# Attention with two expert layers on one core: the second layer's output product in a seven-product block form, made inside the next tile's steps, with part of the weights read from DRAM for every tile

## The chip, the core and the metric

The kernel runs on one core of a Trainium2 chip. The core has TensorE (PE in the tables, with its weight loads as PEld), VectorE (DVE), ScalarE (ACT), GpSimd (POOL), and SyncE (SP), which here only issues transfers. The metric is device microseconds of one execution.

## The reference

```python
# attention: 4 batches, 8 heads, 768 positions, head size 64 (local window plus a few global keys)
x = attention(q, k, v)                               # 3072 tokens x 512
h = maximum(maximum(x @ w1, x @ w2), x @ w3)         # 512 -> 768
x2 = h @ w_out                                       # 768 -> 512
gate = 1 / (1 + exp(-(x2 @ w_gate)))                 # 512 -> 1536
val = x2 @ w_val                                     # 512 -> 1536
out = (gate * val) @ w2_out                          # 1536 -> 512
```

Inputs and output are wide floats. The kernel computes each product with both operands split into two 16-bit parts (high and low), so that one product is three matmuls: high x high, low x high, high x low.

## The kernel before

The first phase does the attention, the first layer, and the conversion of all weights; the result x2 goes to DRAM. The second phase (`phase2`) does the second layer in 6 tiles of 512 tokens, and each tile in 6 steps f, each of which makes 256 of the 1536 middle columns.

A step makes gate and value in the seven-product form of a 2 x 2 block product (Strassen's, in Winograd's arrangement; the table `WINO` names which of seven weight blocks meets which of seven input blocks). The function `prod(n)` in `phase2` makes one of the seven: 12 matmuls of 256 columns into one PSUM bank (2 sides, 2 halves of the contraction, 3 split terms), 84 a step. The products 6, 5, 7, 2, 3, 4 take turns in three banks with the tag `mm`; product 1 has one bank `pv`. VectorE adds each bank into buffers in SBUF (`add`, line 763; seven such additions a step), and a bank is free for the third next product when its addition is done. Then ScalarE makes the sigmoid (790, 794), VectorE multiplies by the value (791, 795), and `split` (line 229) makes the two 16-bit parts: ScalarE casts to the high part (234), VectorE subtracts it to get the low one (243).

The output product is plain: `out_step` adds one step's share into four banks (`tr`, `sc`), with 2 x 4 x 3 = 24 matmuls of 512 columns, and it is placed in the step after. After a tile's sixth step ScalarE scales the four banks (736) and SyncE stores them.

`load_x2` (line 688) makes the seven input blocks of a tile from x2: seven splits and four subtractions (698) of 512 elements on VectorE, seven casts on ScalarE. There are two such buffers, so tile t+2 can be split only when the last matmul of tile t is done. The weights of the second layer are converted in the first phase (`w2_steps`), written to DRAM, and read back once; all 6 steps' weights stay in SBUF for the whole second phase.

The order of the instructions on each engine is made by the framework: it lists them by its own model of their times and emits each when its inputs are ready in that model. On the chip every engine runs its list strictly in that order.

Of the kernel before, what the change touches and what calls it, by code (L numbers as in the profile page):

```python
# [8 lines left out]
F32 = mybir.dt.float32  # L9
# [34 lines left out]
HF2 = NF2 // 2  # L44
Q = 256

# [60 lines left out]
class Fast:  # L107
# [7 lines left out]
    def run(self):  # L115
        tc, nc = self.tc, self.nc
        with ExitStack() as es:
# [4 lines left out]
            self.osum = self.p0.tile([P, NT], F32, name="osum")  # L122
# [169 lines left out]
    def w2_steps(self):  # L292
# [17 lines left out]
        for f in range(HF2):  # L310
            for j in range(2):
# [22 lines left out]
                yield  # L334
            for i in range(2):
                got = []
                yield from made(got)
                w = cv.tile([P, 2, DM], F16, tag="wo", name=f"wo{f}_{i}", bufs=2)
                self.split(w[:, 0], w[:, 1], got[0], "act", "dve")
                if f == 0 and i == 0:  # L340
                    self.least(6, w[:, 0])
                nc.sync.dma_start(out=self.w2d[f, 2 + i], in_=w)
                yield

    def load_w2(self, pool, f):
        for j in range(4):
            shape = [P, 2, 7, Q] if j < 2 else [P, 2, DM]
            self.w2[f, j] = pool.tile(shape, F16, tag=f"w2_{f}_{j}", name=f"w2_{f}_{j}", bufs=1)
            self.nc.sync.dma_start(out=self.w2[f, j], in_=self.w2d[f, j])
# [320 lines left out]
    def phase1_tail(self):  # L670
        n = 0
        for f in range(2):
            self.load_w2(self.p2a, f)
# [42 lines left out]
    def phase2(self):  # L716
        nc, p = self.nc, self.p2b
        for f in range(2, HF2):
            self.load_w2(p, f)
        pend = []  # L720

        def out_step(t, f, gs, acc):
            for i in range(2):
                wo = self.w2[f, 2 + i]
                g = gs[i]
                first, last = f == 0 and i == 0, f == HF2 - 1 and i == 1
                for s in range(4):
                    ss = slice(s * P, (s + 1) * P)
                    for m, (a, b) in enumerate(((g[:, 1, ss], wo[:, 0]), (g[:, 0, ss], wo[:, 1]),
                                                (g[:, 0, ss], wo[:, 0]))):  # L730
                        nc.tensor.matmul(out=acc[s], lhsT=a, rhs=b, start=(first and m == 0),  # L731
                                         stop=(last and m == 2))
                    if last:
                        o = p.tile([P, DM], F32, tag="o", name=f"o{t}_{s}", bufs=4)

                        nc.scalar.activation(out=o, in_=acc[s], func=AF.Copy, scale=1.0 / (XS * WS),
                                             accum_out=self.osum[:, 4 * t + s:4 * t + s + 1])
                        r0 = t * 512 + s * P
                        nc.sync.dma_start(out=self.out[r0:r0 + P, :], in_=o)

        for t in range(NTOK // 512):
            x = self.x2t[t]
            for f in range(HF2):
                if f == 1 and t + 1 < NTOK // 512:
                    self.load_x2(t + 1)

                def prod(n):
# [3 lines left out]
                    for j in range(2):  # L751
                        w = self.w2[f, j]
# [16 lines left out]
                c1, c11, c12, u2, u3, u4 = [sb(tag, bufs=2) for tag in ("c1", "c11", "c12", "u2", "u3", "u4")]  # L769
                c2 = sb("c2", (2, 2, Q), bufs=2)  # L770
                p6 = prod(6)
                p1 = prod(1)
                nc.scalar.copy(out=c1, in_=p1)
                add(u2, p6, c1)
                p5 = prod(5)
                add(u4, p5, u2)
                p7 = prod(7)
                add(c2[:, :, 1], p7, u4)
                add(u3, p7, u2)
                if pend:  # L780
                    out_step(*pend.pop(0))
                add(c11, prod(2), c1)
                add(c12, prod(3), u4)
                add(c2[:, :, 0], prod(4), u3)
                gs = []
                for i in range(2):
                    sg = sb("sg", (2, Q), bufs=3) if i == 0 else sb("sh", (2, Q), bufs=3)
                    if i == 0:
                        for h, y in ((0, c11), (1, c12)):
                            nc.scalar.activation(out=sg[:, h], in_=y[:, 0], func=AF.Sigmoid, scale=1.0 / (XS * GS))  # L790
                            nc.vector.scalar_tensor_tensor(out=sg[:, h], in0=y[:, 1], scalar=1.0 / WS, in1=sg[:, h],
                                                           op0=ALU.mult, op1=ALU.mult)
                    else:
                        nc.scalar.activation(out=sg, in_=c2[:, 0], func=AF.Sigmoid, scale=1.0 / (XS * GS))
                        nc.vector.scalar_tensor_tensor(out=sg, in0=c2[:, 1], scalar=1.0 / WS, in1=sg,
                                                       op0=ALU.mult, op1=ALU.mult)
                    g = p.tile([P, 2, 512], F16, tag=f"g{i}", name=f"g{t}_{f}_{i}", bufs=2)
                    self.split(g[:, 0].rearrange("p (h q) -> p h q", h=2), g[:, 1].rearrange("p (h q) -> p h q", h=2),
                               sg, "act", "dve")
                    gs.append(g)  # L800
# [283 lines left out]
```

## Time and profile before

| | |
|---|---|
| median of 3 runs | 1133.11 us (1130.88 to 1134.29) |
| profiled execution: time, span | 1131.62 us, 1129.8 us |
| PE busy | 1066.4 us, 94% of the span |
| PEld / DVE busy | 866.9 us (77%) / 786.9 us (70%) |
| ACT / POOL busy | 569.4 us (50%) / 252.9 us (22%) |
| moved by DMA | 104.04 MB, mean 92 GB/s |

The shares are averages over the two phases: POOL works in the first phase alone, and the second phase begins near 602 us of the span. Matmuls are pipelined, so a busy PE is read by the distance between the starts of its matmuls, not by its busy share alone.

### The profile page before, as it was taken

Reading aid. Unit: us, or ns where it says so; the run is one execution under the profiler, and the core shown is the slowest. Engines: PE = TensorE matmul, PEld = TensorE weight load, DVE = VectorE, ACT = ScalarE, POOL = GpSimd, SP = SyncE. Lnnn points to the kernel's source line nnn. Section 1 sums busy time; section 2 is a strip of 40 time slices with the busy share of each in tenths; the row PEclk is TensorE's granted clock in tenths of the full one; section 3 lists DMA queues with packets and bytes.
Section 4 is the critical chain, followed back from the end, with each engine's and each line's share of the span. In section 5 each row is a group of like instructions: output and inputs, shape, how many; then the busy total and the mean of one; then the engine's idle time right before and its main releaser. Section 6 shows DMA issues by size and latency. Waiting matters only on the chain.

```text
span 1129.8 us, 23579 instructions
## 1 busy us (share of the span) xinstructions
PE 1066.4 (94%) x9219; PEld 866.9 (77%) x9219; DVE 786.9 (70%) x1907; ACT 569.4 (50%) x1432; POOL 252.9 (22%) x385
## 2 busy tenths in 40 slices
PE   4678788999999999999999999999999999999996
PEld 3567667998998888988988777777777777777773
DVE  7999997668988888988537457557557556545553
ACT  6887776557877777776434124224224224223222
POOL 7343344333644444544310000000000000000000
PEclk9699999999999999999999999999999999999999
DMA  9625546444554554221248202002002001001001
GB/s 239 170 68 149 150 142 202 144 147 146 161 150 145 151 164 124 90 81 50 85 141 323 106 1 75 1 1 76 1 1 75 1 1 39 1 1 39 1 1 41
DMA packets 123575, 104.04 MB, mean 92 GB/s; under 512 B 78816, under 2 KB 106464, under 8 KB 123456
## 3 DMA queue, kind: packets, MB, share of 16 engines
q1 hardware_dynamic: 116544, 96.16, 28.5%
q10 hardware_dynamic: 6912, 6.29, 1.6%
q8 instruction: 74, 1.21, 0.5%
q14 instruction: 45, 0.37, 0.1%
HBM read 70.78 MB, written 26.74 MB: 86 GB/s over the span
## 4 chain that ended last, share of the span: by engine, by line
PE 59%; DVE 6%; ACT 3%; issue 2%; DMA 1%; POOL 0%; ACTq 0%; DVEq 0%; POOLq 0%
PE mm L757 25%; PE mm L568 11%; PE tr L731 8%; PE sc L731 8%; PE pv L757 4%; PE tr L509 1%; PE pv L534 1%; DVE ht L589 1%; ACT sp L484 1%; DVE xs L546 1%; DVE nx L101 1%; DVE nx L103 1%; DVE x L243 0%; DMA x2r<-x2d 0%; PE sc L469 0%
## 5 line engine op out<-in xcount | busy, mean ns | idle before, releaser
L568 PEld LDWEIGHTS <-w 128*128 128x128 f16 x3456 | 333.3, 98 | 54.2 <-issue 8.7
L757 PEld LDWEIGHTS <-w 128*128 128x128 f16 x3024 | 295.9, 98 | 44.6 <-issue 0.9
L568 PE MATMUL mm<-xt,w 128*128 128x256 f16 x2592 | 317.1, 274 | 9.3 <-DVE ht L589 3.4
L757 PE MATMUL mm<-x,w 128*128 128x256 f16 x2592 | 302.4, 273 | 0.5 <-DVE u L763 0.5
L790 ACT ACTIVATE sg<-c 128x256 f32<-128x256 f32 x72 | 30.0, 416 | 314.7 <-DVE c L763 314.7
L731 PEld LDWEIGHTS <-g 128*128 128x128 f16 x864 | 84.4, 98 | 95.3 <-DVE g L243 2.9
L763 DVE TENSOR_TENSOR c<-mm,c 128x512 f32<-128x512 f32 x36 | 24.9, 692 | 168.1 <-PE mm L757 168.1
L497 POOL TENSOR_SCALAR sp<-sp,rc 128x256 f32<-128x256 f32 (+1 forms) x192 | 109.9, 589 | 54.9 <-DVE rc L493 43.7
L568 PE MATMUL mm<-hh,w 128*128 128x256 f16 x864 | 108.1, 273 | 4.3 <-DVE ht L589 1.4
L731 PE MATMUL tr<-w,g 128*128 128x512 f16 x432 | 105.0, 379 | 2.7 <-DVE g L243 2.7
L731 PE MATMUL sc<-w,g 128*128 128x512 f16 x432 | 105.0, 379 | 0.0
L484 ACT ACTIVATE sp<-sp,mn 128x256 f32<-128x256 f32 (+1 forms) x192 | 92.3, 483 | 20.0 <-DVE mn L480 15.3
L763 DVE TENSOR_TENSOR c<-mm,u 128x512 f32<-128x512 f32 x108 | 74.3, 689 | 23.4 <-PE mm L757 21.4
L589 DVE SCALAR_TENSOR_TENSOR ht<-mm,ht 128x256 f32<-128x256 f32 x144 | 60.1, 418 | 33.4 <-PE mm L568 23.9
L243 POOL TENSOR_TENSOR hh<-ht,hh 128x256 f16<-128x256 f32 x72 | 55.9, 778 | 110.1 <-ACT hh L234 109.9
L512 DVE TENSOR_TENSOR pt<-tr,pt 128x512 f16<-128x512 f32 (+1 forms) x96 | 61.5, 641 | 19.4 <-ACT pt L511 18.3
L480 DVE CUSTOM_DVE_ANT_0 sp<-sc,b 128x256 f32<-128x256 f32 (+1 forms) x192 | 68.6, 393 | 5.3 <-PE sc L469 3.7
L243 POOL TENSOR_TENSOR xt<-xs,xt 128x256 f16<-128x256 f32 x48 | 36.3, 757 | 151.0 <-ACT xt L234 151.0
L534 PEld LDWEIGHTS <-vt 128*128 128x128 f16 x704 | 52.3, 102 | 21.3 <-issue 12.2
L509 PE MATMUL tr<-ident,sp 128*128 128x128 f32 x352 | 60.8, 286 | 7.5 <-POOL sp L497 4.1
L757 PE MATMUL pv<-x,w 128*128 128x256 f16 x432 | 62.4, 273 | 0.0
L511 ACT CAST pt<-tr 128x512 f16<-128x512 f32 (+1 forms) x96 | 52.2, 543 | 8.2 <-PE tr L509 7.0
(135 smaller groups left out, 1437.1 us busy)
## 6 DMA issues: line engine op xcount, KB each, us to landing
w2d<-wu SPq DMA_DIRECT2D x12, 896.0 KB, 3.9
w<-w2d SPq DMA_DIRECT2D x12, 896.0 KB, 7.8
rw<-in_moe_w_dram SPq DMA_DIRECT2D x18, 512.0 KB, 5.2
rw<-in_moe_w_out_dram SPq DMA_DIRECT2D x18, 512.0 KB, 3.9
rawk<-in_k_dram SPq DMA_DIRECT2D x24, 256.0 KB, 4.8
rawq<-in_q_dram SPq DMA_DIRECT2D x24, 256.0 KB, 3.8
rawv<-in_v_dram SPq DMA_DIRECT2D x24, 256.0 KB, 4.7
rw<-in_moe_w_gate_dram SPq DMA_DIRECT2D x12, 512.0 KB, 3.6
```

Source lines behind the costliest of these rows:

```text
L243: e.tensor_tensor(out=lo, in0=src, in1=hi, op=ALU.subtract)
L480: nc.vector.tensor_tensor_reduce(out=sp[:, u], in0=sc[:, u], in1=bias, scale=-SCALE / (QS * QS), scalar=3.0e38, op0=ALU.add, op1=ALU.min, ...
L484: nc.scalar.activation(out=sp[:, u], in_=sp[:, u], func=AF.Exp, scale=-1.0, bias=self.mn[:, r, u:u + 1], accum_out=self.sum[:, r, u, 0:1])
L497: nc.gpsimd.tensor_scalar(out=sp[:, u], in0=sp[:, u], scalar1=self.rc[:, m % 4, u:u + 1], scalar2=PS_, op0=ALU.mult, op1=ALU.mult)
L509: nc.tensor.transpose(tr[:, u, c], sp[:, u, c], self.ident)
L512: nc.vector.tensor_tensor(out=pt[:, 1], in0=tr, in1=pt[:, 0], op=ALU.subtract)
L534: nc.tensor.matmul(out=pv[:, u], lhsT=a, rhs=b, start=(m == 0), stop=(m == len(mms) - 1))
L568: nc.tensor.matmul(out=ps, lhsT=a, rhs=b, start=(m == 0), stop=(m == len(seq) - 1))
L589: self.recent = nc.vector.scalar_tensor_tensor(out=t, in0=ps, scalar=1.0 / WS, in1=prev[blk], op0=ALU.mult, op1=ALU.max).ins
L731: nc.tensor.matmul(out=acc[s], lhsT=a, rhs=b, start=(first and m == 0), stop=(last and m == 2))
L757: nc.tensor.matmul(out=ps[:, j], lhsT=w[:, a, sw, ks], rhs=x[:, b, sx, k], start=(m == 0), stop=(m == 5))
L763: nc.vector.tensor_tensor(out=out, in0=ps, in1=b, op=ALU.add)
```

## The change

The output product of a tile is now made in the seven-product form as well. The middle result of each step goes into seven blocks: one from the first two token halves directly, two from the second half, four sums. `ga` and `gb` hold the sigmoid products, GpSimd makes the four sums (`sum_`, line 875 of the changed kernel, 256 elements each), and `split` makes high and low parts of all seven (`gw`). The weights `w2_out` are brought into seven blocks in `w2_steps`, with four subtractions on GpSimd, and written to `wod` in DRAM.

The generator `output(t, gw)` makes tile t's seven output products. Each is 6 steps x 2 row halves x 3 terms = 36 matmuls of 256 columns into one bank, 252 a tile. They run in tile t+1: two products each after its steps f = 0, 1, 2 and one after f = 3; those of the last tile run at the end, two of them begun early. VectorE adds them into the output tiles (line 785, seven times a tile), and two stores a tile take the place of four; ScalarE then sums each stored half (line 815, 1024 elements).

All steps' results of a tile now have to be kept until the next tile, so the weights of steps 2 to 5 no longer stay in SBUF: `load_w2` reads them for every tile into a ring of three slots, and `load_wo` reads each of the seven output blocks (768 KB) for every tile into three slots. The additions of a step use fewer buffers, in place.

```diff
+WRB = 3
+WOB = 3
+ORDER = (6, 1, 5, 7, 3, 2, 4)
+STEPS = {0: (0, 1), 1: (2, 3), 2: (4, 5), 3: (6,)}
...
+            sub(sm[:, 0], a[:, Q:], a[:, 0:Q])
+            sub(sm[:, 1], b[:, Q:], sm[:, 0])
+            yield
+            sub(sm[:, 2], b[:, Q:], a[:, Q:])
+            sub(sm[:, 3], b[:, 0:Q], sm[:, 1])
...
+            self.split(w[:, 0, 0], w[:, 1, 0], a[:, 0:Q], "act", "dve")
+            self.split(w[:, 0, 1:3], w[:, 1, 1:3], b.rearrange("p (s c) -> p s c", s=2), "act", "dve")
+            yield
+            for i in (0, 2):
+                self.split(w[:, 0, 3 + i:5 + i], w[:, 1, 3 + i:5 + i], sm[:, i:i + 2], "act", "dve")
...
-                self.split(w[:, 0], w[:, 1], got[0], "act", "dve")
...
+        for j in range(2):
+            pool, tag, bufs = (self.p2a, f"w2_{f}_{j}", 1) if f < 2 else (self.p2b, f"wr{j}", WRB)
+            w = pool.tile([P, 2, 7, Q], F16, tag=tag, name=f"w2_{t}_{f}_{j}", bufs=bufs)
...
-        def out_step(t, f, gs, acc):
-            for i in range(2):
-                wo = self.w2[f, 2 + i]
-                g = gs[i]
-                first, last = f == 0 and i == 0, f == HF2 - 1 and i == 1
-                for s in range(4):
-                    ss = slice(s * P, (s + 1) * P)
-                    for m, (a, b) in enumerate(((g[:, 1, ss], wo[:, 0]), (g[:, 0, ss], wo[:, 1]),
-                                                (g[:, 0, ss], wo[:, 0]))):
-                        nc.tensor.matmul(out=acc[s], lhsT=a, rhs=b, start=(first and m == 0),
-                                         stop=(last and m == 2))
...
+            def prod(i, fs):
+                n = ORDER[i]
+                a, b = SLOTS[WINO[n][0]]
+                if fs[0] == 0:
+                    ps[n] = self.bank(("tr", "sc")[i % 2], [P, 2, Q])
+                for f in fs:
+                    for u in range(2):
+                        us = slice(u * P, (u + 1) * P)
+                        for m, (x, y) in enumerate(((0, 0), (1, 0), (0, 1))):
+                            nc.tensor.matmul(out=ps[n][:, u], lhsT=gw[f][a][:, x, b, us], rhs=wos[t, i][:, f, y],
...
+                if fs[-1] == HF2 - 1:
+                    load_wo(t, i + WOB)
...
+            def add(out, n, b):
+                nc.vector.scalar_tensor_tensor(out=out, in0=ps[n], scalar=step, in1=b, op0=ALU.mult, op1=ALU.add)
...
+                if f >= 2 and ring.index((t, f)) + WRB < len(ring):
+                    self.load_w2(*ring[ring.index((t, f)) + WRB])
...
+                sum_(sm[:, 0], ga[:, 1], gb[:, 1], ALU.add)
+                sum_(sm[:, 1], sm[:, 0], ga[:, 0])
+                sum_(sm[:, 2], ga[:, 0], ga[:, 1])
+                sum_(sm[:, 3], gb[:, 0], sm[:, 1])
...
+                for y, src in zip(g, (ga[:, 0:1], gb, sm[:, 0:2], sm[:, 2:4])):
+                    self.split(y[:, 0], y[:, 1], src, "act", "dve")
...
+                if out is not None:
+                    for _ in STEPS.get(f, ()):
+                        next(out)
...
+            out = output(t, gw, first=(0, 1) if t == tiles - 1 else ())
```

Three places in the order of instructions follow. The names are tiles: `x_1`, `x_3` are input blocks and `x2r` their raw data, `mm` the banks of a step's products, `c` the step's buffers (`u` too, before), `o` the output tiles; the first number behind `c`, `g`, `ga`, `gb`, `gw` is the step.

VectorE at the start of the second phase, before the change: the first additions of tile 0 (line 763) stand among the splits of tile 1's input.

```order
L698 TENSOR_TENSOR x2r_10030<-x2r_10030 128x2x256
L243 TENSOR_TENSOR x_1_10032<-x2r_10030,x_1_10032 128x512
L816 MEMSET bad 128x4
L819 TENSOR_SCALAR huge<-tot 128x60
L698 TENSOR_TENSOR x2r_10030<-x2r_10030 128x2x256
L763 TENSOR_TENSOR u_0_9907<-mm_9911,c_0_9904 128x512
L822 TENSOR_REDUCE bad<-wmx 128x1
L820 TENSOR_SCALAR huge<-huge 128x60
L243 TENSOR_TENSOR x_1_10032<-x2r_10030,x_1_10032 128x512
L698 TENSOR_TENSOR x2r_10030<-x2r_10030 128x2x256
L763 TENSOR_TENSOR u_0_9909<-mm_9939,u_0_9907 128x512
```

The same place in the changed kernel.

```order
L725 TENSOR_TENSOR x2r_10048<-x2r_10048 128x2x256
L251 TENSOR_TENSOR x_1_10050<-x2r_10048,x_1_10050 128x512
L904 MEMSET bad 128x4
L907 TENSOR_SCALAR huge<-tot 128x60
L910 TENSOR_REDUCE bad<-wmx 128x1
L251 TENSOR_TENSOR x_1_10050<-x2r_10048,x_1_10050 128x512
L908 TENSOR_SCALAR huge<-huge 128x60
L911 TENSOR_SCALAR bad<-bad 128x1
L845 TENSOR_TENSOR c_0_9921<-mm_9922,c_0_9919 128x2x256
L909 TENSOR_REDUCE bad<-huge 128x1
L845 TENSOR_TENSOR c_0_9920<-mm_9950,c_0_9921 128x512
```

All of tile 1's splits and subtractions now stand ahead of the first addition (line 845), where four of them stood behind it.

VectorE from tile 0's last step into tile 1, before: the splits and subtractions of tile 2's input, and the first step's additions.

```order
L795 SCALAR_TENSOR_TENSOR sh_5_10765<-c_5_10633,sh_5_10765 128x512
L243 TENSOR_TENSOR g_5_0_10762<-sg_5_10757,g_5_0_10762 128x512
L698 TENSOR_TENSOR x2r_10933<-x2r_10933 128x2x256
L763 TENSOR_TENSOR u_0_10774<-mm_10778,c_0_10771 128x512
L243 TENSOR_TENSOR x_2_10935<-x2r_10933,x_2_10935 128x512
L243 TENSOR_TENSOR g_5_1_10768<-sh_5_10765,g_5_1_10768 128x512
L698 TENSOR_TENSOR x2r_10933<-x2r_10933 128x2x256
L763 TENSOR_TENSOR u_0_10776<-mm_10806,u_0_10774 128x512
L243 TENSOR_TENSOR x_2_10935<-x2r_10933,x_2_10935 128x512
L698 TENSOR_TENSOR x2r_10933<-x2r_10933 128x2x256
L763 TENSOR_TENSOR c_0_10777<-mm_10820,u_0_10776 128x2x256
L763 TENSOR_TENSOR u_0_10775<-mm_10820,u_0_10774 128x512
```

The same kind of place in the changed kernel, from tile 1's last step into tile 2.

```order
L845 TENSOR_TENSOR c_5_11680<-mm_11753,c_5_11680 128x512
L871 SCALAR_TENSOR_TENSOR ga_5_11785<-c_5_11679,ga_5_11785 128x256
L871 SCALAR_TENSOR_TENSOR ga_5_11785<-c_5_11680,ga_5_11785 128x256
L251 TENSOR_TENSOR gw_5_0_11798<-ga_5_11785,gw_5_0_11798 128x256
L845 TENSOR_TENSOR c_5_11681<-mm_11767,c_5_11681 128x2x256
L251 TENSOR_TENSOR x_3_12023<-x2r_12021,x_3_12023 128x512
L154 TENSOR_REDUCE chk<-x_3_12023 128x1
L251 TENSOR_TENSOR x_3_12023<-x2r_12021,x_3_12023 128x512
L845 TENSOR_TENSOR c_0_11812<-mm_11813,c_0_11810 128x2x256
L725 TENSOR_TENSOR x2r_12021<-x2r_12021 128x2x256
L251 TENSOR_TENSOR x_3_12023<-x2r_12021,x_3_12023 128x512
L871 SCALAR_TENSOR_TENSOR gb_5_11786<-c_5_11681,gb_5_11786 128x512
```

The stretch begins with the same work as before, but the additions now belong to steps that have no output product on TensorE between them, and each step brings more splits (`gw`, line 251).

SyncE at the very end, before: the last stores.

```order
L739 DMA out_dram<-o_3_14480 128x512
L739 DMA out_dram<-o_0_15280 128x512
L739 DMA out_dram<-o_1_15286 128x512
L739 DMA out_dram<-o_2_15292 128x512
L739 DMA out_dram<-o_3_15298 128x512
L1050 TENSOR_LOAD flag
```

The same end in the changed kernel.

```order
L757 DMA wo_0_15667<-wod 128x3072
L757 DMA wo_1_15707<-wod 128x3072
L812 DMA out_dram<-o_0_15209 128x2x512
L757 DMA wo_2_15877<-wod 128x3072
L812 DMA out_dram<-o_1_15210 128x2x512
L757 DMA wo_3_16207<-wod 128x3072
L757 DMA wo_4_16215<-wod 128x3072
L757 DMA wo_5_16256<-wod 128x3072
L757 DMA wo_6_16296<-wod 128x3072
L812 DMA out_dram<-o_0_16137 128x2x512
L812 DMA out_dram<-o_1_16138 128x2x512
```

Five loads of output weights now stand between and ahead of the stores; `wo_3` can start only when the product that uses `wo_0` is done.

## Rows read from the trace of the kernel before

**Rows 1.** Stretches: start:end, length, then busy us (and count) by engine, clock, DMA share, GB/s.

```profile
300.00:400.00 100.00, 99.61 (x1011) 90.15 (x1008) 85.45 (x248) 78.03 (x215) 46.62 (x71) 1.00 0.56 162
800.00:900.00 100.00, 100.00 (x754) 73.58 (x753) 56.21 (x98) 27.44 (x57) 0.00 (x0) 1.00 0.07 22
```

**Rows 2.** Timeline of TensorE near the end: start, length, line, operation, count, idle before.

```profile
1080.81 4.09 PE L757 MATMUL mm<-x,w 128*128 128x256 f16 x36
1084.74 0.49 PE L757 MATMUL pv<-x,w 128*128 128x256 f16 x3
...
1089.98 1.46 PE L731 MATMUL tr<-w,g 128*128 128x512 f16 x6
...
1092.57 1.46 PE L731 MATMUL tr<-w,g 128*128 128x512 f16 x6
...
1116.38 1.47 PE L731 MATMUL tr<-w,g 128*128 128x512 f16 x6 [2.67 <-DVE g L243]
```

**Rows 3.** Groups of VectorE by form in the second phase and in load_x2.

```profile
L763 DVE TENSOR_TENSOR c<-mm,u 128x512 f32<-128x512 f32 x108 | 74.3, 689 | 23.4 <-PE mm L757 21.4
...
L791 DVE SCALAR_TENSOR_TENSOR sg<-c,sg 128x256 f32<-128x256 f32 x72 | 30.3, 421 | 17.4 <-ACT sg L790 17.4
L243 DVE TENSOR_TENSOR x<-x2r,x 128x512 f16<-128x512 f32 x42 | 29.2, 703 | 5.9 <-ACT x L234 5.8
...
L795 DVE SCALAR_TENSOR_TENSOR sh<-c,sh 128x512 f32<-128x512 f32 x36 | 24.9, 691 | 10.8 <-ACT sh L794 10.7
...
L243 DVE TENSOR_TENSOR g<-sg,g 128x512 f16<-128x512 f32 x36 | 24.6, 684 | 0.1
```

**Rows 4.** Single lines, durations in ns min/median/max: GpSimd's sums, two of VectorE.

```profile
L319 POOL TENSOR_TENSOR sm<-nx x12: 718/724/1111, 186.5 to 495.7; 128x256 f32<-128x256 f32 x12
...
L243 DVE TENSOR_TENSOR wu<-sm,wu x12: 678/685/1162, 209.1 to 503.0; 128x512 f16<-128x512 f32 x12
...
L512 DVE TENSOR_TENSOR pt<-tr,pt x96: 409/684/693, 23.3 to 563.4; 128x512 f16<-128x512 f32 x80, 128x256 f16<-128x256 f32 x16
```

**Rows 5.** Groups of VectorE by form in the first phase.

```profile
L243 DVE TENSOR_TENSOR w<-nx,w 128x512 f16<-128x512 f32 x24 | 19.0, 795 | 0.0
...
L243 DVE TENSOR_TENSOR wu<-sm,wu 128x512 f16<-128x512 f32 x12 | 8.4, 734 | 0.0
```

**Rows 6.** Groups of ScalarE by form.

```profile
L790 ACT ACTIVATE sg<-c 128x256 f32<-128x256 f32 x72 | 30.0, 416 | 314.7 <-DVE c L763 314.7
...
L794 ACT ACTIVATE sh<-c 128x512 f32<-128x512 f32 x36 | 22.7, 629 | 18.2 <-DVE c L763 18.2
```

**Rows 7.** Timeline of all engines from the first phase's end into the second.

```profile
594.85 0.41 DVE L589 SCALAR_TENSOR_TENSOR ht<-mm,ht 128x256 f32<-128x256 f32 x1
...
595.78 1.21 POOL L243 TENSOR_TENSOR hh<-ht,hh 128x256 f16<-128x256 f32 x1 [4.14 <-ACT hh L234]
595.78 1.76 DVE L243 TENSOR_TENSOR x<-x2r,x 128x512 f16<-128x512 f32 x2
...
602.38 4.09 PE L757 MATMUL mm<-x,w 128*128 128x256 f16 x36
602.68 1.66 ACT L234 CAST x<-x2r 128x512 f16<-128x512 f32 x3 [2.22 <-DMA x2r<-x2d]
...
608.49 1.47 PE L757 MATMUL mm<-x,w 128*128 128x256 f16 x12 [0.51 <-DVE u L763]
```

**Rows 8.** One stretch, columns as in the first group: the second phase's weights are being read.

```profile
600.00:605.00 5.00, 5.00 (x48) 4.48 (x46) 1.67 (x4) 2.33 (x5) 0.00 (x0) 1.00 1.05 420
```

**Rows 9.** Transfers by kind: queue, count, KB each, median us from issue to landing.

```profile
w<-w2d SPq DMA_DIRECT2D x12, 896.0 KB, 7.8
...
words<-in_n_global_dram SPq DMA_DIRECT2D x1, 1.0 KB, 2.6
```

**Rows 10.** Timeline behind the last matmul of the output product.

```profile
1121.77 0.60 ACT L736 ACTIVATE o<-sc 128x512 f32<-128x512 f32 x1
1122.27 0.19 ACT L736 ACTIVATION_READ_ACCUMULATOR o<-sc 128x1 f32 x1
```

More of the change, by code (lines that the diff above doesn't have):

```diff
@@ L741, in phase2, with load_wo @@
-        for t in range(NTOK // 512):
+        tiles = NTOK // 512
+        ring = [(t, f) for t in range(tiles) for f in range(2, HF2)]
+        for q in ring[:WRB]:
+            self.load_w2(*q)
+        wos = {}
+        def load_wo(t, i):
+            if i >= len(ORDER):
+                t, i = t + 1, i - len(ORDER)
+            if t < NTOK // 512:
+                w = p.tile([P, HF2, 2, Q], F16, tag="wo", name=f"wo{t}_{i}", bufs=WOB)
+                nc.sync.dma_start(out=w, in_=self.wod[WINO[ORDER[i]][1]])
+                wos[t, i] = w
@@ L742, in phase2, with store @@
+        def store(t, h, o):
+            r0 = t * 512 + h * Q
+            nc.sync.dma_start(out=self.out[r0:r0 + Q, :].rearrange("(u p) d -> p u d", p=P), in_=o)
+            junk = p.tile([P, 2, DM], BF16, tag="junk", name=f"junk{t}_{h}", bufs=1)
+            nc.scalar.activation(out=junk, in_=o, func=AF.Copy, accum_out=self.osum[:, 2 * t + h:2 * t + h + 1])
+        for i in range(WOB):
+            load_wo(0, i)
+        out = None
+        for t in range(tiles):
             x = self.x2t[t]
+            gw = []
@@ L785, in phase2 @@
[L785 to L800, printed above, removed]
+                add(c22, p7, c12)
@@ new lines, in phase2, with sum_ @@
+                sm = sb("sm", (4, Q))
+                def sum_(out, a, b, op=ALU.subtract):
+                    nc.gpsimd.tensor_tensor(out=out, in0=a, in1=b, op=op)
+                sum_(sm[:, 0], ga[:, 1], gb[:, 1], ALU.add)
+                sum_(sm[:, 1], sm[:, 0], ga[:, 0])
+                sum_(sm[:, 2], ga[:, 0], ga[:, 1])
+                sum_(sm[:, 3], gb[:, 0], sm[:, 1])
+                g = [p.tile([P, 2, 1 if i == 0 else 2, Q], F16, tag=f"gw{i}", name=f"gw{t}_{f}_{i}",
+                            bufs=HF2 + 1 + LASTS[i]) for i in range(4)]
@@ L1008, in attention_moe @@
     x2d = dram.tile([DM, NTOK], F32, name="x2d")
-    w2d = {(f, j): dram.tile([P, 2, 7, Q] if j < 2 else [P, 2, DM], F16, name=f"w2d_{f}_{j}")
-           for f in range(HF2) for j in range(4)}
+    w2d = {(f, j): dram.tile([P, 2, 7, Q], F16, name=f"w2d_{f}_{j}")
+           for f in range(HF2) for j in range(2)}
+    wod = dram.tile([7, P, HF2, 2, Q], F16, name="wod")
     cst = ctx.enter_context(tc.tile_pool(name="cst", bufs=1, side="right"))
```

121 lines of the change are left out of this document (75 added, 46 removed).

## The prediction

> **What bounds the kernel now.** I read first the stretches, to see which engine is full in which phase. In the second phase TensorE is busy all the time and VectorE a little over half, GpSimd not at all; in the first phase TensorE is nearly full and VectorE at 85% with GpSimd at 47% [rows 1]. So the second phase ends by TensorE, and the distance between the starts of its matmuls is the price. The timeline near the end gives it: 36 matmuls of 256 columns start within 3.93 us, 0.1092 us each; 12 of 512 columns within 2.59 us, 0.2158 us each [rows 2]. A step is 84 x 0.1092 + 24 x 0.2158 = 9.17 + 5.18 = 14.35 us. Only at the very end does TensorE wait, 2.67 us for the last split [rows 2]. Then I read VectorE's groups, since its work grows, and the first phase for GpSimd and VectorE side by side, which the second phase of before never shows.
>
> **Matmuls.** A tile's output product was 144 x 0.2158 = 31.1 us and becomes 252 x 0.1092 = 27.5 us: 3.56 us a tile, **21.4 us** in six. That the new matmuls also take 0.1092 us I read from the step's products, which have the same shape and one weight load each; that loads then fill nine tenths of the time is no obstacle, since the first phase runs so with TensorE at 99.6% [rows 1]. The Trainium skill (TensorE: Matmul & The Clock Gate, section Back-to-back issue gap) gives a sustained 131 ns at 512 columns and 81 ns at 128, so wide matmuls would be far cheaper per column; with some 98 ns between them for 256 as an estimate the change would cost 24.7 - 18.9 = 5.8 us a tile, 35 us. The trace disagrees: 215.8 ns, in step with 109.2.
>
> **VectorE per step.** Seven additions of 0.69, three multiplications (0.42, 0.42, 0.69) as before; the splits were two of 0.68 and become three of 0.68 and one of 256 elements, for which I take the 0.42 of the other instructions of that width [rows 3]: 4.83 + 1.53 + 2.47 = 8.83 us. TensorE's step without an output product is 9.17 us. So wherever steps follow each other without output products (all of tile 0; steps 4, 5 and the next 0 later) VectorE is 96% full before it waits for anything. In steps 0 to 3 output products make TensorE's step 13 to 17 us, and nothing is short there: the seven additions of the output tile (0.69 each) lie in that slack.
>
> Two things come on top. First, a wait: the multiplication needs ScalarE's sigmoid, 0.42 or 0.63 us [rows 6], behind the step's last addition. In the order of the changed kernel the next step's first addition (0.69) sometimes stands in between and sometimes not, so 0 to 0.7 us a step; I take 0.4. Second, GpSimd's four sums a step, 0.724 us each when alone [rows 4]. Where GpSimd and VectorE both work on SBUF, both stretch: a GpSimd instruction takes 1.21 us and two splits 1.76 instead of 1.37 [rows 7]; single ones reach 1111 and 1162 ns, while an instruction of VectorE with one input from PSUM never exceeds 693 ns [rows 4]. The Trainium skill (SBUF — State Buffer, section Who interferes with whom) says the same: a VectorE instruction with two SBUF inputs and a reading GpSimd instruction lock each other out, whole instructions long; the trace agrees. Seven instructions of a step are of that kind (three multiplications, four splits). On average such ones cost 734 and 795 ns in the first phase [rows 5], 0.05 to 0.11 above 0.685, so 0.35 to 0.77 us a step; GpSimd was 47% busy there [rows 1] and will be a third, so I take b = 0.4. Outer bounds: nothing, and 4 x 0.48 = 1.9 us if each sum holds up VectorE by the longest stretch seen.
>
> **Tile 0.** Tile 1's raw input came at 602.7, 5.1 us after tile 0's last split ended at 597.5 [rows 7]. In the new order that split stands ahead of the addition that ran at 594.85, so the data should land near 600. But all eleven splits and subtractions (0.70 each, 7.7 us) and some 1 us of small ones now stand ahead of the first addition: near 608.7. From there to the last addition of step 5: 42 additions (29.0), 17 multiplications (8.5), 20 splits (12.4), 0.4 of checks, 50.3 us, and 6 x (0.4 + b) = 4.8: 663.8. TensorE unhindered has started at 602.4 and ends these 510 matmuls after 55.7 us, its last addition at 658.8. It is held up 5.0 us through its three banks; 0.5 of such a wait exists before [rows 7]. **+4.5.**
>
> **Four tile changes with an input to split** (into tiles 1 to 4). VectorE has three steps (26.5), the splits (7.7), an output addition and checks (1.1), 35.2 us, and 3 x (0.4 + b) = 2.4; TensorE 3 x 9.17 + 72 x 0.1092 = 35.4. VectorE ends 2.2 us late, of which TensorE bears about 1: going through the listed rows with these durations from step 4's last addition on, the bank for product 4 of the new tile is free 1.0 us, and the low part that the first output product needs 0.5 us, before TensorE comes to it. 1.2 us each, **+4.8**. Before, the same splits are hidden, because TensorE has 14.35 us a step.
>
> **End.** The 2.67 us wait goes: the last tile's seven products keep TensorE going while step 5's blocks are made (some 61 matmuls, 6.7 us, against a chain of about 5 us: an addition, the sigmoid, a multiplication, two sums, cast, split). In its place comes a load: `wo_3` may start when the product on `wo_0` ends, and only 15 matmuls and a transpose (1.9 us) lie between. A transfer of 1 KB lands after 2.6 us [rows 9], and 786 kB at 420 GB/s [rows 8] are 1.9: 4.5 and 0.3 to issue, 2.9 us of wait. **+0.2.** Behind the last matmul there was one ScalarE instruction of 0.60 with 0.19 [rows 10]; now an addition (0.69) and a sum over 1024 elements, by the slope of 416 to 629 ns [rows 6] about 1.06: **+1.15.**
>
> **First phase.** `w2_steps` gains 1.1 us of splits and four GpSimd sums (3 us) for each of six weight pairs. TensorE loses only 0.4 of 100 us there [rows 1], so most of it hides behind TensorE; if the cover fails, 6.6 us of VectorE come out. I take **+1.5** (0 to 5).
>
> **Sum.** -21.4 + 4.5 + 4.8 + 0.2 + 1.15 + 1.5 = -9.3 us on the profiled 1131.62: 1122.4. The median of the runs shown is 1.5 above that execution, so 1123.
>
> **Rivals.**
> - All of VectorE's lateness is absorbed, by banks and buffers, as in the tile changes of before, and the first phase doesn't change: -21.4 + 1.35 - 0.5, about 1111. For it speaks that VectorE is at 56% in the second phase now [rows 1]; against it that 96% of a step leaves no room for any wait.
> - VectorE becomes the bound, and the kernel is slower. My sum of stalls is 2.1 + 18 b (6 steps in tile 0, 3 in each of four changes); with 18.55 us of net gain the point is b = 0.91 us of blocking a step. At b = 1.4 it is 1140, and at the outer bound of 1.9, with each of the four sums holding VectorE up by 0.48, 1149. The Trainium skill (SBUF — State Buffer, section Who interferes with whom) lets the one that comes second wait out the whole other instruction, which leads to that end. Against it: GpSimd's last three sums depend on a multiplication after which VectorE's list goes on with additions from PSUM, which do not collide.
> - The weights come late. 1.8 MB a step and 5.5 MB of output blocks a tile are about 155 GB/s, against 420 [rows 8]. The shortest cover is step 5 of tile 0: 127 matmuls, 13.9 us from the freed slot to the first use, against 7.8 us to landing [rows 9]. If queueing doubled that, 1.7 us a tile, 10 us: 1132, no change.
> - Narrow matmuls cost more per column than wide ones, by 35 us in all, as the Trainium skill's figures have it (TensorE: Matmul & The Clock Gate, section Back-to-back issue gap): 1166. The rows at both widths speak against it [rows 2].
>
> **Chances.** Forecast 0.61 (1116 to 1130), full gain 0.15, VectorE as bound 0.18, late weights 0.05, TensorE's rule 0.01. A change of 0.3% (3.4 us) is about what this kernel's runs can tell from none. Faster: the full gain and the forecast but for 0.06 at its upper end, 0.70. Same: that 0.06, a part of VectorE as bound near its point (0.05), and late weights, 0.15 in all after rounding. Slower: the rest, 0.15. The range runs from the full gain to VectorE as bound just past its point: 1111 to 1137.
>
> **What would show it.** In the second phase's stretches: TensorE full at 0.1092 us a matmul in steps 0 to 3; waits of it for VectorE (line 845) adding to 4 to 6 us in tile 0 and about 1 at each change into tiles 1 to 4, none into tile 5; VectorE's multiplications and splits (lines 871, 251) at 0.72 to 0.80 instead of 0.69, its additions unchanged; one wait of about 3 us for `wo` at the end. The prediction is wrong if these waits are above 18 us in all or near zero, if TensorE waits for a load inside the tiles, or if the first phase ends more than 5 us later or earlier than 602.

## The result, and the profile after

The changed kernel takes **1113.66 us** (median of 4 runs, 1112.39 to 1113.90) against 1133.01 (1130.88 to 1134.29) before: ratio **0.983** (95% interval 0.981 to 0.985), 19.4 us less. The forecast was 1123, in a range of 1111 to 1137: the sign is right and the time lies in the range, near its lower end, but the gain is twice the one that was worked out.

The two profiled executions differ by 17.7 us of span (1129.8 and 1112.1). Three marks split this: the first product of the second phase ([rows 7] before, 607.92 after), and the end of the last output matmul, 1121.74 before (where ScalarE's instruction of [rows 10] begins, 0.03 later) and 1102.62 after.

| part | before | after | difference | forecast |
|---|---|---|---|---|
| first phase | 602.38 | 607.92 | +5.5 | +1.5 |
| second phase to the last matmul | 519.4 | 494.7 | -24.7 | -11.9 |
| behind the last matmul | 8.1 | 9.5 | +1.4 | +1.15 |

The stretches of the changed kernel, columns as in [rows 1], the first from the first phase:

```profile
300.00:400.00 100.00, 96.29 (x968) 86.38 (x966) 80.35 (x234) 74.09 (x201) 52.06 (x80) 1.00 0.51 144
800.00:900.00 100.00, 100.00 (x919) 89.64 (x917) 73.73 (x123) 37.03 (x70) 23.96 (x28) 1.00 0.53 189
```

In the second phase TensorE stays full while VectorE goes from 56% to 74%, GpSimd from nothing to 24%, and the transfers from 22 to 189 GB/s. In the first phase TensorE falls from 99.6% [rows 1] to 96.3%. What TensorE waited for in the second phase, up to the last output matmul (engine, line, releaser, us in total, times, longest):

```profile
PE pv L839 <- ACT c L855: 0.4, 1, 0.4
```

This one wait of 0.4 us, for ScalarE, stands at the very start of tile 0, where 9 us of waits for VectorE in tile 0 and at the tile changes had been forecast. One step of tile 0 on VectorE shows why (start, length, line, operation, count, idle before):

```profile
644.38 0.69 DVE L845 TENSOR_TENSOR c<-mm,c 128x512 f32<-128x512 f32 x1 [0.27 <-PE mm L839]
644.99 0.41 DVE L871 SCALAR_TENSOR_TENSOR ga<-c,ga 128x256 f32<-128x256 f32 x1
645.55 0.42 DVE L871 SCALAR_TENSOR_TENSOR ga<-c,ga 128x256 f32<-128x256 f32 x1 [0.15 <-ACT ga L870]
645.90 0.69 DVE L845 TENSOR_TENSOR c<-mm,c 128x512 f32<-128x512 f32 x1
646.50 0.57 DVE L251 TENSOR_TENSOR gw<-ga,gw 128x256 f16<-128x256 f32 x1
647.34 0.69 DVE L871 SCALAR_TENSOR_TENSOR gb<-c,gb 128x512 f32<-128x512 f32 x1 [0.27 <-ACT gb L870]
647.95 0.68 DVE L845 TENSOR_TENSOR c<-mm,c 128x512 f32<-128x512 f32 x1
648.72 0.69 DVE L251 TENSOR_TENSOR gw<-gb,gw 128x512 f16<-128x512 f32 x1
649.33 0.68 DVE L845 TENSOR_TENSOR c<-mm,c 128x512 f32<-128x512 f32 x1
650.27 1.29 DVE L845 TENSOR_TENSOR c<-mm,c 128x512 f32<-128x512 f32 x2 [0.26 <-PE mm L839]
651.48 1.28 DVE L251 TENSOR_TENSOR gw<-sm,gw 128x512 f16<-128x512 f32 x2
652.68 0.69 DVE L845 TENSOR_TENSOR c<-mm,c 128x512 f32<-128x512 f32 x1
653.66 0.69 DVE L845 TENSOR_TENSOR c<-mm,c 128x512 f32<-128x512 f32 x1 [0.29 <-PE mm L839]
```

Read the starts, not the lengths. 651.48 to 652.68 are two instructions of 512 elements, shown with 0.68 each, but they take 1.20 us from start to start of the next: **0.60 us each**. One of 256 elements, shown with 0.41 to 0.42, takes 0.35 here (645.55 to 645.90) and 0.335 to 0.342 in the median over the trace. The end of one overlaps the beginning of the next. So a step without output products is not 8.83 us of VectorE but 7 x 0.60 + (2 x 0.335 + 0.60) + (0.335 + 3 x 0.60) = **7.6 us**, 83% of TensorE's 9.17. VectorE is the one that waits: the step shown runs 9.3 us, from 644.38 to 653.66, so some 1.7 us of it are waits and stretched instructions; 1.0 us of that the rows put down to waits for TensorE and ScalarE.

The end, against [rows 2, 10] before:

```profile
1078.11 4.09 PE L775 MATMUL sc<-wo,gw 128*128 128x256 f16 x36
1082.04 4.75 PE L775 MATMUL tr<-wo,gw 128*128 128x256 f16 x42
1086.63 0.27 PE L913 MATMUL pv<-ident,chk 128*43 128x128 f32 x1
1086.74 4.09 PE L775 MATMUL sc<-wo,gw 128*128 128x256 f16 x36
...
1098.53 4.09 PE L775 MATMUL tr<-wo,gw 128*128 128x256 f16 x36
...
1102.66 0.69 DVE L785 SCALAR_TENSOR_TENSOR o<-tr,o 128x512 f32<-128x512 f32 x1 [3.24 <-PE tr L775]
...
1103.44 1.06 ACT L815 ACTIVATE junk<-o 128x1024 bf16<-128x1024 f32 x1 [2.84 <-DVE o L785]
```

Neither the wait of 2.67 us nor the forecast one for `wo_3` is there: the product on that block begins at 1086.74, right behind a small transpose. 36 matmuls start within 3.93 us, 0.1092 each, as the step's products did before.

In the first phase TensorE waits more, and for other things. From 210 to 602 us, first before and then after:

```profile
PE pv L534 <- DMA vt<-vg: 1.5, 3, 0.7
PE sc L469 <- DMA qb<-qa: 1.4, 1, 1.4
PE tr L509 <- POOL sp L497: 0.7, 2, 0.4
PE mm L568 <- ACT x2o L610: 0.2, 1, 0.2
```

```profile
PE pv L561 <- DMA vt<-vg: 2.5, 2, 1.6
PE mm L595 <- ACT ht L614: 1.5, 4, 0.5
PE mm L595 <- ACT x2o L637: 1.3, 3, 0.6
PE mm L595 <- POOL hh L251: 1.2, 3, 0.7
PE sc L495 <- DVE kr L499: 1.1, 1, 1.1
PE mm L595 <- ACT xt L242: 0.6, 1, 0.6
PE mm L595 <- POOL xt L251: 0.4, 1, 0.4
```

3.8 us became 8.6, in waits of at most 1.6 us for all three other engines and for transfers. The four engines' lists are the same in both kernels up to 188 us on VectorE and to between 213 and 217 us on the others, about where the first output weights come in, and the times there differ by 0.1 us; the loss comes behind that.

### The profile page after: what moved, and what is told of

Its sections match the earlier page's. It is cut to its first block, busy times and chain, and to the rows that moved or that the text cites. A ratio compares the mean times of both kernels' runs of the same rounds, so it can differ in the third digit from the quotient of the medians.

```text
span 1112.1 us, 25427 instructions
## 1 busy us (share of the span) xinstructions
PE 1042.6 (94%) x9867; PEld 928.1 (83%) x9867; DVE 864.1 (78%) x2033; ACT 613.9 (55%) x1498; POOL 397.2 (36%) x553
## 4 chain that ended last, share of the span: by engine, by line
PE 49%; DVE 3%; ACT 1%; POOL 1%; issue 1%; DMA 0%; ACTq 0%; DVEq 0%; POOLq 0%
PE mm L839 25%; PE tr L775 8%; PE sc L775 6%; PE mm L595 4%; PE pv L839 4%; DVE x L251 1%; DMA x2r<-x2d 0%; DVE x2r L725 0%; DVE ht L616 0%; PE pv L561 0%; POOL sp L524 0%; ACT sp L511 0%; PE tr L536 0%; DVE wmx L419 0%; DVE wu L251 0%
## 5 line engine op out<-in xcount | busy, mean ns | idle before, releaser
L595 PE MATMUL mm<-xt,w 128*128 128x256 f16 x2592 | 312.6, 273 | 13.6 <-DVE ht L616 4.2
L845 DVE TENSOR_TENSOR c<-mm,c 128x512 f32<-128x512 f32 x252 | 169.0, 686 | 51.4 <-PE mm L839 24.5
L775 PEld LDWEIGHTS <-gw 128*128 128x128 f16 x1512 | 148.0, 98 | 17.1
L875 POOL TENSOR_TENSOR sm<-ga 128x256 f32<-128x256 f32 x36 | 29.3, 814 | 306.2 <-DVE ga L871 306.2
L775 PE MATMUL tr<-wo,gw 128*128 128x256 f16 x864 | 108.5, 273 | 0.0
L870 ACT ACTIVATE ga<-c 128x256 f32<-128x256 f32 x72 | 30.0, 417 | 127.7 <-DVE c L845 127.3
L775 PE MATMUL sc<-wo,gw 128*128 128x256 f16 x648 | 75.3, 273 | 0.0
L242 ACT CAST gw<-sm 128x512 f16<-128x512 f32 x72 | 44.4, 617 | 49.9 <-POOL sm L875 49.9
L251 DVE TENSOR_TENSOR gw<-sm,gw 128x512 f16<-128x512 f32 x72 | 49.2, 692 | 25.4 <-ACT gw L242 23.9
```

The lines of the kernel that those rows point to most:

```text
L251: e.tensor_tensor(out=lo, in0=src, in1=hi, op=ALU.subtract)
L595: nc.tensor.matmul(out=ps, lhsT=a, rhs=b, start=(m == 0), stop=(m == len(seq) - 1))
L775: nc.tensor.matmul(out=ps[n][:, u], lhsT=gw[f][a][:, x, b, us], rhs=wos[t, i][:, f, y], start=(f == 0 and u == 0 and m == 0), stop=(f == H ...
L845: nc.vector.tensor_tensor(out=out, in0=ps, in1=b, op=ALU.add)
```

## Experiments

**1. How much room does VectorE have?** Theory A: what counts is the distance between starts, so there is over 1 us of room a step. Theory B, its rival: the shown durations add up, and the changed kernel had just none left.

`sums_dve`, the four sums moved to VectorE:

```diff
-                    nc.gpsimd.tensor_tensor(out=out, in0=a, in1=b, op=op)
+                    nc.vector.tensor_tensor(out=out, in0=a, in1=b, op=op)
```

> The changed kernel with the four sums of each step on VectorE instead of GpSimd. Theory A (VectorE begins back-to-back instructions 0.60 us apart at 512 elements and 0.335 us at 256, although each is shown 0.69 and 0.42 long, so a step without output products is 7.6 us of VectorE against 9.17 us of TensorE): four sums more are 4 x 0.335 = 1.34 us, 8.9 to 9.15 us a step, still within TensorE's 9.17; TensorE waits 0 to 4 us in all and the time is 1113 to 1118. Theory B (the shown durations add, 8.83 us a step, and the changed kernel had just no room left): 4 x 0.42 = 1.7 us more in each of some 18 steps, 25 to 30 us, about 1140.

Measured: 1114.11 us (ratio 0.984, 0.982 to 0.987). `extra2` works two low parts out again, `extra4` twice over (with `* 2` in the first line):

```diff
+                for y, src in ((g[1], gb), (g[2], sm[:, 0:2])) * 1:
+                    nc.vector.tensor_tensor(out=y[:, 1], in0=src, in1=y[:, 0], op=ALU.subtract)
                 gw.append(g)
```

> The changed kernel with two more 512-element subtractions of VectorE a step (two low parts are worked out twice, with the same result). Theory A (0.60 us apart): 1.2 us more a step, 8.8 to 9.0 against 9.17; 0 to 3 us in all, 1113 to 1117. Theory B (durations add): 1.37 us more in each of some 18 steps, 25 us, about 1138.

> The changed kernel with four more 512-element subtractions of VectorE a step (two low parts are worked out three times). Theory A: 7.6 + 2.4 + 0.2 of blocking = 10.2 us a step; 1.03 us over TensorE's 9.17 in six steps of tile 0 makes 6 us, and at each of the four changes into tiles 1 to 4 three steps with the splits of the next input make 38.3 against 35.4, 2.9 us each, 12 us; together some 17 us, 1131 (1122 to 1136). TensorE's waits for the additions stand in tile 0 and at the changes. Theory B: 2.8 us in each of some 18 steps, 50 us, about 1163.

Measured: 1114.80 us (0.984, 0.982 to 0.986) and 1119.41 (0.989, 0.986 to 0.991). B falls: even four more instructions a step, 50 us by its sum, cost 5.7 us. One stretch of the second phase in `sums_dve` and in `extra4`:

```profile
700.00:800.00 100.00, 100.00 (x918) 89.64 (x917) 79.82 (x149) 37.03 (x70) 0.00 (x0) 1.00 0.53 187
```

```profile
700.00:800.00 100.00, 99.32 (x909) 88.64 (x908) 95.25 (x159) 38.21 (x72) 30.80 (x32) 1.00 0.50 182
```

TensorE is still full with VectorE at 80%, and 99.3% busy with VectorE at 95%. But A's own sum, 17 us, was too large for `extra4` as well. TensorE's waits there in the second phase:

```profile
PE tr L775 <- DMA wo<-wod: 1.8, 1, 1.8
PE sc L775 <- DMA wo<-wod: 0.9, 1, 0.9
PE mm L839 <- DVE c L845: 0.7, 2, 0.5
```

For the additions it waits 0.7 us, not 17. At the end VectorE's last splits come late, the products that free the slots with them, and two loads of output weights behind those: 2.7 us. Another 1.5 us lie in the first phase, which ended at 609.4 in this execution; its lists are those of the changed kernel, and over five kernels with these lists its end lies between 607.2 and 609.7. The remaining microsecond was not followed up.

So being 1 us a step behind doesn't stop TensorE. Two things in the trace took up what A counted as lateness. The splits lag: when the last addition of tile 0 begins, 40 of its 48 splits (`gw`, lines 251 and 886) are done, in the changed kernel 20 of 24. And the list of `extra4` is another one: the framework placed some 54 of tile 0's own output matmuls (5.9 us) between the steps of tile 0, some 10 in the changed kernel, so these steps are not without output products, as A took them to be, nor does all of a tile's output run in the next one. One such row:

```profile
640.86 1.25 PE L775 MATMUL sc<-wo,gw 128*128 128x256 f16 x10
```

How much each of the two saved was not measured. `extra8` asks whether it is the sum over a tile that counts:

> The changed kernel with eight more 512-element subtractions of VectorE a step (two low parts are worked out five times). Theory C (VectorE may fall behind by splits whose results are read a tile later, and catches up while output products run, so that only the sum over a tile counts): VectorE has 6 x (7.6 + 4.8 + 0.2) + 7 x 0.6 = 79.8 us a tile and 7.7 for the next input in five of them, 517 us in all, against 495 of TensorE; 22 us and some 5 at the start, about 1140 (1132 to 1148). Theory D (each step must keep up by itself): 3.6 us too much in six steps of tile 0, and 10.7 at each of four changes, 65 us, about 1179.

Measured: 1167.78 us (1.031, 1.029 to 1.033). One stretch of it, and TensorE's longest waits in the second phase:

```profile
664.00:764.00 100.00, 92.33 (x828) 79.94 (x826) 99.19 (x172) 35.14 (x71) 28.15 (x28) 1.00 0.52 180
```

```profile
PE tr L775 <- DVE gw L886: 10.2, 5, 3.6
PE tr L775 <- ACT gw L242: 8.2, 8, 2.3
PE mm L839 <- DVE c L845: 5.8, 11, 1.3
```

Now VectorE is the bound: from 613 us to its last split, which ends near 1137, it is 98% busy, and from 664 to 1064 over 99%. These are 524 us, where theory C had 517. TensorE waits above all for blocks of the output product, less for free banks. C's 1140 left out that after the last split some 18 us of output products still stand alone (to 1155.7); with those it comes to about 1158, and with the 7 us that VectorE took longer to 1165. D's 1179 is 11 us too high. C describes where VectorE's limit is; as a time neither forecast held.

**2. Is a narrow matmul dearer per column?** `narrow`, in the kernel before:

```diff
-                        nc.tensor.matmul(out=acc[s], lhsT=a, rhs=b, start=(first and m == 0),
-                                         stop=(last and m == 2))
+                        for q in range(2):
+                            qs = slice(q * Q, (q + 1) * Q)
+                            nc.tensor.matmul(out=acc[s][:, qs], lhsT=a, rhs=b[:, qs], ...)
```

> The kernel before with each output matmul of 512 columns cut into two of 256, with as many weight loads as matmuls. By the spacing in the rows (0.1092 us at 256 columns, 0.2158 at 512) a tile has 288 x 0.1092 - 144 x 0.2158 = 0.37 us more, 2.2 us in six tiles: 1135. If a narrow matmul cost more per column, the time goes up with it. By the Trainium skill (TensorE: Matmul & The Clock Gate, section Back-to-back issue gap), with 131 ns at 512 columns and some 98 ns as an estimate at 256, it would be 9.4 us a tile, 56 us.

Measured: 1134.47 us, ratio 1.0019 (1.0008 to 1.0030): 2.2 us, as the two rows said. In the profiled executions the second phase, from its first product to the end of the last output matmul, takes 521.6 us against 519.4. The timeline in a tile:

```profile
804.96 1.47 PE L733 MATMUL tr<-w,g 128*128 128x256 f16 x12
806.27 1.47 PE L733 MATMUL sc<-w,g 128*128 128x256 f16 x12
```

From the one row to the next 12 matmuls start, in 1.31 us, 0.1092 each.

**3. Do the reloaded weights cost anything?** `ring`, in the kernel before: steps 2 to 5 take their hidden-layer blocks from three slots that are filled anew for every tile.

```diff
+                if f >= 2 and ring.index((t, f)) + 3 < len(ring):
+                    load_ring(*ring[ring.index((t, f)) + 3])
```

> The kernel before with one part of the change alone: the hidden-layer weight blocks of steps 2 to 5 come from DRAM again for every tile, three slots deep, instead of once. Theory H (the transfers are hidden, TensorE never waits for one): no change, 1131 to 1135, with some 130 GB/s more in the second phase. Rival L (they come late, or slow other work by contention): TensorE's waits for them, or longer instructions, 1.7 us a tile and more, 1143 and up.

Measured: 1135.01 us, ratio 1.0015 (1.0004 to 1.0026). The profile shows no cause for 1.7 us: its span is 1129.4 (before: 1129.8), TensorE waits for no load in the second phase, and it is at 100% with 103 GB/s in the stretch from 700 to 800, where the kernel before moves 29; so the reloading adds some 74 GB/s, not the 130 expected. But the profiled execution is the fastest of the twelve, and its second phase is 0.7 us longer (520.0), with one more wait of 0.5 us for an addition. The transfers are hidden from TensorE; whether the ratio's small excess comes from them stays open. The output blocks, which the changed kernel reads besides, are not in this run; in the changed kernel's own trace TensorE waits for no load in the second phase, at 189 GB/s.

**4. What makes the first phase longer?** Theories G (GpSimd's subtractions), V (the splits) and O (the changed order), with four kernels. `nosub` leaves the four subtractions out, `nosplit` makes two splits where four are needed:

```diff
-            sub(sm[:, 0], a[:, Q:], a[:, 0:Q])
-            sub(sm[:, 1], b[:, Q:], sm[:, 0])
...
-            sub(sm[:, 2], b[:, Q:], a[:, Q:])
-            sub(sm[:, 3], b[:, 0:Q], sm[:, 1])
...
```

```diff
-            self.split(w[:, 0, 0], w[:, 1, 0], a[:, 0:Q], "act", "dve")
-            self.split(w[:, 0, 1:3], w[:, 1, 1:3], b.rearrange("p (s c) -> p s c", s=2), "act", "dve")
+            self.split(w[:, 0, 0:2], w[:, 1, 0:2], a.rearrange("p (s c) -> p s c", s=2), "act", "dve")
             yield
-            for i in (0, 2):
-                self.split(w[:, 0, 3 + i:5 + i], w[:, 1, 3 + i:5 + i], sm[:, i:i + 2], "act", "dve")
+            self.split(w[:, 0, 2:4], w[:, 1, 2:4], sm[:, 2:4], "act", "dve")
...
```

> The changed kernel without the four GpSimd subtractions of each output weight pair in the first phase; the splits that used them read the unsummed rows instead, so the output weights are not the combined ones. The first phase ended at 602.4 us before and at 607.9 in the changed kernel. Theory G (the added subtractions make GpSimd late for the softmax scaling and the low parts behind it): the first phase ends near 603 to 604, the time falls by some 4 us to about 1109.5. Theory V (the added casts and splits of ScalarE and VectorE do it) and theory O (only the changed order of the list does it): 607 to 609.5, 1113 to 1115.

> The changed kernel with only two 512-element splits for each output weight pair in the first phase, as many as before, in place of one of 256 and three of 512 elements; the subtractions stay, and parts of the output weights are stored twice over, so they are not the combined ones. Theory V: the first phase ends near 603 to 605, the time is about 1109 to 1111. Theories G and O: 607 to 609.5, 1113 to 1115.

`p1dve` has `nc.vector` for `nc.gpsimd` in the new subtractions, `p1dve_all` in all twelve sums of `w2_steps`:

> The changed kernel with the four subtractions of each output weight pair in the first phase on VectorE instead of GpSimd. They are 24 instructions of 256 elements, 0.335 us apart, 8 us of VectorE over 350. Theory G: the first phase ends at 603 to 605, the time is about 1109 to 1111. Theory V (VectorE is what the added work delays): 609 to 613, 1115 to 1118. Theory O: 607 to 609.5.

> The changed kernel with all sums of the second layer's weights in the first phase (twelve a step of the hidden width, 72 instructions of 256 elements) on VectorE instead of GpSimd: 24 us of VectorE over 350, and some 53 us less of GpSimd. Theory G: the first phase ends at 600 to 604, the time is 1106 to 1110. Theory V: VectorE, shown busy 83% of this stretch, is late for the banks, 612 to 622, 1118 to 1128.

`spread` and `spread2` let the pieces out more slowly. The diff is that of `spread`; `spread2` has `2 if n % 3 else 1` there, and in `phase1_tail` a piece at every fourth instead of every sixth group:

```diff
-                    self.behind(2)
+                    self.behind(2 - n % 2)
```

> The changed kernel with the conversion of the second layer's weights let out more slowly: one and two pieces by turns instead of two at each step of the attention loop, so that some 30 of the 144 pieces fall into the last 45 us of the first phase, where VectorE, ScalarE and GpSimd are little used. Theory S (the first phase is longer because the added pieces crowd those three engines while the attention runs): the first phase ends at 603 to 606 instead of 607.9, and the time is 1109 to 1112. Rival: the late pieces, or the stores behind them, hold up the start of the second phase, 609 or later, 1115 and up.

> The changed kernel with the conversion of the second layer's weights let out a little more slowly, two pieces at two of three steps of the attention loop and one at the third, and the rest a piece every fourth matmul group behind it, so that 17 of the 144 pieces follow the attention and all are done before the splits of tile 0's input begin. The attention's last product stood at 573.7 us in the changed kernel, at 568.2 before, at 566.4 with 30 pieces left over. Theory S (crowding during the attention, and a loss behind it only where pieces meet the input's splits): the attention ends at 568 to 572, the first phase at 603 to 606, no wait of some 5 us at the start of the second phase, and the time is 1109 to 1112. Rival (17 pieces behind the attention cost there what they saved): 607 and later, 1113 and up.

| kernel | start of the attention's last group of products | end of the first phase | median us | ratio to before (95%) |
|---|---|---|---|---|
| before, `narrow`, `ring` | 567.5 to 568.2 | 601.7 to 602.4 | | |
| changed, and four with its lists there | 573.0 to 575.5 | 607.2 to 609.7 | 1113.66 | 0.9829 (0.9812 to 0.9846) |
| `nosub` | 571.9 | 606.1 | 1111.26 | 0.9810 (0.9792 to 0.9827) |
| `nosplit` | 571.2 | 605.6 | 1110.66 | 0.9802 (0.9785 to 0.9819) |
| `p1dve` | 572.2 | 606.5 | 1112.50 | 0.9827 (0.9809 to 0.9845) |
| `p1dve_all` | 573.2 | 607.4 | 1115.21 | 0.9851 (0.9830 to 0.9872) |
| `spread` | 566.4 | 608.1 | 1118.37 | 0.9867 (0.9848 to 0.9886) |
| `spread2` | 568.8 | 605.4 | 1110.51 | 0.9797 (0.9784 to 0.9811) |

Neither G nor V holds alone. Taking out the subtractions or half of the splits ends the first phase 1 to 2 us before the earliest of the five executions with the changed kernel's lists, not at 602 to 604; the medians are 2.4 and 3.0 us lower, with intervals that overlap that of the changed kernel. Moving sums to VectorE wins nothing that is clear of noise. O can't be taken out alone: each of these kernels has an order of its own. What does move the end of the attention is the preparation that runs beside it. That is 132 pieces before (the code has 22 for each of six steps), 144 in the changed kernel, 127 in `spread2` and some 114 in `spread`; with the last two the attention ends as early as before, at 568.8 and 566.4, and TensorE's waits up to its end, 3.8 us before and 8.6 in the changed kernel, fall to 4.1 and 3.4. So the loss is crowding on three engines whose lists run in strict order, and it can be taken away. Whether it takes a lower density or fewer pieces, these runs don't show, since the last two kernels have both, fewer even than before. Part of the loss comes back behind the attention. In `spread` that is all of it and more, by the rival that was named. TensorE's two longest waits from 590 to 640 us:

```profile
PE pv L839 <- ACT c L855: 5.6, 1, 5.6
PE mm L595 <- DVE ht L616: 2.4, 1, 2.4
```

The last pieces met the splits of tile 0's input on VectorE. So its raw buffer came free late, and tile 1's data were loaded at 606.85 instead of 599.83. ScalarE's casts of these data stood in its list ahead of the copy that frees the `pv` bank, and TensorE waited 5.6 us for that copy. In `spread2` all pieces are done before those splits begin: 1110.51 us, 3.2 below the changed kernel (the two intervals just don't overlap), though not to be told from `nosplit`, which does less work. In the profile 2.2 us of waits for VectorE (`ht`) still stand behind the attention.

## Why the prediction came out so

The time lies in the forecast range partly by luck. Two of the three signs by which the prediction called itself wrong have come: the waits for VectorE are near zero, and the first phase ends 5.5 us later. The two errors have opposite signs; with the forecast's +1.5 in the first phase instead of +5.5 the time would, as an estimate, have been about 1110, just below the range. Term by term:

- **Matmuls, -21.4: right.** 0.1092 us each, TensorE at 100%. The rival by which narrow matmuls cost more per column has fallen (`narrow`: 2.2 us forecast from rows, 2.2 measured). The same section of the Trainium skill (TensorE: Matmul & The Clock Gate, section Back-to-back issue gap) also has a formula, columns / 2.4 + 2.5 ns, which it keeps for isolated matmuls; it gives 109 and 216, and the trace agrees with it in a full stream.
- **VectorE per step, 8.83 us: this step failed.** The sum added durations of instructions that follow each other directly, and these overlap. The step is 7.6 us. The stalls of tile 0 (+4.5) and of the four tile changes (+4.8) were worked out from this; measured are one wait of 0.4, as short as the 0.5 of before, and none. A sign of it stood in [rows 7], for ScalarE: three casts in 1.66 us, where one instruction of that width takes 0.63 [rows 6].
- **Each microsecond of lateness is a stall** (2.1 + 18 b): failed too, as `extra4` shows. TensorE needs the additions in time, since they free its three banks; most splits are read a tile later, and they lag (by 8 of 48 at the end of tile 0 in `extra4`), while the list gave TensorE some 54 output matmuls within that tile. VectorE only decides when its work over a tile exceeds TensorE's (`extra8`). The rival with VectorE as the bound was real in kind, but its point lies between four and eight more instructions a step, 2.4 to 4.8 us, not at b = 0.91.
- **Blocking, b = 0.4: right in kind, too large.** With the sums on GpSimd the multiplication of `gb` takes 839 ns on average, with them on VectorE 688:

```profile
L871 DVE SCALAR_TENSOR_TENSOR gb<-c,gb 128x512 f32<-128x512 f32 x36 | 30.2, 839 | 12.7 <-ACT gb L870 12.7
```

```profile
L871 DVE SCALAR_TENSOR_TENSOR gb<-c,gb 128x512 f32<-128x512 f32 x36 | 24.8, 688 | 0.8 <-ACT gb L870 0.8
```

The first row is of the changed kernel, the second of `sums_dve`. With the smaller differences of the other splits and multiplications it makes about 0.23 us a step. The additions, with one input from PSUM, have 686 and 685.

- **End, +0.2: -2.67.** The wait for the split went as forecast. The wait for `wo_3` didn't come, because its load didn't wait for the product on `wo_0`, as the text ahead of the prediction and the prediction have it: it was issued at 1082.24, when the product on `wo_1` had ended, and landed at 1086.39, 0.35 us before its own product began.
- **Behind the last matmul, +1.15: +1.4.** The addition (0.69) and the sum (1.06) are as forecast.
- **First phase, +1.5 (0 to 5): +5.5, and 5 to 7 in other executions.** Mis-sized: TensorE losing 0.4 of 100 us was taken for cover, but with the added pieces its waits for the other engines and transfers in this phase grew from 3.8 to 8.6 us.
- **Sum.** In the second phase the rival of the full gain, with a chance of 0.15, is what happened; the first phase took 5.5 of it back. Matmuls 21.4 and the end's wait 2.67 explain 24.1 of the 24.7; the remaining 0.6 was not followed up. The late weights fell too: no wait for a load inside a tile. The sum itself has a slip: 1122.4 and 1.5 make 1123.9, not 1123.

## What to carry to other kernels

For an engine that may become the bound, take the distance between the starts of two instructions that follow each other directly, not the sum of their durations; a merged row gives it at once (x2 in 1.28 us, where one is shown with 0.68). Then ask what of its work someone needs at once and what may lag: here the rest had to fit the sum over a tile, not each step. And where a change adds preparation to a stretch with lists in strict order, a full main engine is no proof of cover: let out more slowly, so that 17 of the 144 pieces came behind that stretch but before the next stretch's own preparation, the same work took 3.2 us less.

## What was unexpected of the hardware

Back-to-back VectorE instructions start 0.60 us apart at 512 elements per partition and 0.335 at 256, in every kernel here, whether inputs come from PSUM or SBUF, though each is shown some 0.08 longer. The Trainium skill has this (Vector Engine (DVE) Microarchitecture Reference, section Measured stream behaviour on trn2): 1.0417 ns per column and some 75 ns an instruction after overlap, 608 and 342 ns as an estimate; the trace agrees, with 8 ns less at either width. That page would have corrected the prediction's largest error.

In `spread` TensorE's clock fell after the wait of 5.6 us. Its timeline, and the granted clock (third column from the end) in stretches of 4 us:

```profile
617.77 2.72 PE L839 MATMUL pv<-x,w 128*128 128x256 f16 x12 [5.58 <-ACT c L855]
620.28 2.77 PE L839 MATMUL mm<-x,w 128*128 128x256 f16 x12
622.84 1.28 PE L839 MATMUL pv<-x,w 128*128 128x256 f16 x6
623.96 1.47 PE L839 MATMUL mm<-x,w 128*128 128x256 f16 x12
```

```profile
616.00:620.00 4.00, 2.23 (x11) 1.61 (x11) 4.00 (x11) 2.02 (x5) 0.00 (x0) 0.62 1.01 423
620.00:624.00 4.00, 4.00 (x22) 2.87 (x21) 3.75 (x8) 2.41 (x4) 0.00 (x0) 0.53 1.02 427
624.00:628.00 4.00, 4.00 (x39) 3.57 (x37) 2.38 (x6) 1.45 (x4) 0.78 (x1) 1.00 1.03 420
```

Twelve matmuls start within 2.51 us, 0.21 each, until the clock is back from the lower level (1.2 GHz) to the upper (2.4): the 30 from 617.77 to 623.96 take 6.2 us, where 0.1092 each would be 3.3, some 2.9 us more on top of the wait. So this execution of `spread` lost over 8 us at one place. It took 1122.11 us; the other three took 1117.81 to 1118.46 at a higher mean granted clock (0.982 to 0.990 against 0.975), and no profile shows how much of this loss they had.
